# Gate/value passes on two row halves over 128 columns instead of four quarters of the array

## The chip, the cores and the metric

The kernel runs on one core of a Trainium2 chip. A core has TensorE (matrix products; the profile shows its matmuls as PE and its weight loads as PEld), VectorE (DVE), ScalarE (ACT), GpSimd (POOL) and SyncE (SP), which run side by side and wait for each other by semaphores. The metric is device time in microseconds (us) for one execution. Smaller is better.

## The reference, cut to what matters

There are 8 batches, 12 heads, 448 rows and a head dimension of 64. Squared-ReLU attention is followed by a gated feed-forward layer of width 1536.

```python
scores = scale * np.matmul(q, k.transpose(0, 1, 3, 2))      # per batch and head: 448 x 448
attn   = np.maximum(scores, 0.0) ** 2 / S
x      = np.matmul(attn, v)                                  # -> 3584 rows x 768
gate   = np.maximum(x @ w_gate, 0.0)                         # 768 x 1536
val    = x @ w_val
out    = gate * val @ w_out                                  # 1536 x 768
```

The kernel works in bf16 with sums in fp32.

## The kernel before

**One batch after the other, two in a pair.** For each batch the kernel makes three kinds of products: score tiles (21 of them, each two 64-row strips of keys of four heads against 448 queries), value products (3, of 7 steps each) and gate/value units (12, one for each block of 128 of the 1536 columns). For each pair of batches `out_pair` then makes the output product. The last pair's gate/value work is another function, `gv_pair`, which forms sums of blocks first and needs fewer products.

**How a product lies in the array.** TensorE holds a stationary operand of up to 128 rows by 128 columns and streams the moving operand past it. A head has only 64 elements, so two row halves of the array do different work: rows 0 to 63 belong to one half of the partitions, rows 64 to 127 to the other. `mm4` (L79) cuts the columns in two as well. For each row half `r` and column half `c` it issues one matmul of 64 rows by 64 columns, so one *pass* is four weight loads and four matmuls, one for each quarter of the array:

```python
for r, p in HALVES:
    for c, half in HALVES:
        mm(o[r][half], lhs(r, c)[p], rhs(r, c)[p], start, stop)
```

The two row halves write to two different PSUM banks `o[0]` and `o[1]`, the two column halves to partitions 0 to 63 and 64 to 127 of each. Scores (`tile_of`, L242), values (`value_passes`), gate/value units (`gv_unit`, L302) and `gv_pair` (L500) all use `mm4`. In scores and values the two column halves hold different weights and also stream different data (`c` picks another pair of heads). In a gate/value pass both column halves stream the same `x`, and their weights are two neighbouring blocks of 64 columns.

**A gate/value unit** fills two banks: one with the gate, one with the value, each 128 columns by 448 rows of `x`. Partitions 0 to 63 of the weights `gv_sb` hold `w_gate`, partitions 64 to 127 hold `w_val`. `x` exists twice, with even and odd heads exchanged between the halves of the partitions, so that each weight half meets each head. That gives 12 passes (6 pairs of heads, twice), each over all 448 rows of `x`. After the last pass ScalarE takes the ReLU of the gate bank and VectorE multiplies it with the value bank.

**Other shapes of the array.** The output products (`out_pair`, L355), the transposes of the first two batches (L208, L217) and the idle matmuls at the start use 128 rows by 64 columns, two matmuls side by side.

**The order of TensorE's work** is written out: every instruction is kept in program order. `spread` (L702) runs through the passes of the 12 units of one batch and puts *events* between them: score tiles and value products of the next batch, placed by `paced` (L740) at even distances. So a gate/value stretch of a few passes alternates with one score tile (one pass of four matmuls) or one value product (seven passes). `first_batch` (L609) has an order of its own, written out by hand, in which score tiles, transposes, value products and the first gate/value passes alternate. ScalarE and VectorE turn each score tile into squared ReLU (L232, L233).

Of the kernel before, what the change touches and what calls it, by code (L numbers as in the profile page):

```python
# [16 lines left out]
def kernel(  # L17
# [24 lines left out]
    B, H, S, D = q.shape  # L42
# [23 lines left out]
    HALVES = [(c, slice(c * 64, c * 64 + 64)) for c in range(2)]  # L66

    def pin(ins):
        return tc.keep_in_program_order(ins)

    def mm(o, l, r, start, stop):
        pin(nc.tensor.matmul(o, lhsT=l, rhs=r, start=start, stop=stop, skip_group_check=True))  # L72
# [6 lines left out]
    def mm4(o, lhs, rhs, start, stop):  # L79
# [4 lines that stand above are left out]
# [10 lines left out]
    def pair_of(b, slot):  # L94
        qd, c = divmod(slot, 2)
        return slot if b == 0 else qd + c * NQ
# [205 lines left out]
    def gv_unit(b, mf, order, take):  # L302

        hT = hT_of[b - b % 2]
        c0 = CHUNK_OF[mf]
        w = gv_sb[c0]
        f = mf * 128 - CHUNKS[c0][0]
        col = (b % 2) * S
        o = []

        def step(n, e, hp):
            if n == 0:
                ps = take()
                o.extend(ps[:, r, :S] for r in range(2))
            x = x_of[b][e][hp // 2]
            mm4(o, lambda r, c: w[:, 2 * pair_of(b, hp) + (r ^ e), f + c * 64:f + c * 64 + 64], lambda r, c: x[:, hp % 2, :],
                n == 0, n == H - 1)
            if n == H - 1:
                g_sb = gpool.tile([128, S], BF16, name="g_sb")
                pin(nc.scalar.activation(g_sb, o[0], AF.Relu, scale=float(out_scale)))  # L320
                pin(nc.vector.tensor_tensor(hT[:, mf, col:col + S], o[1], g_sb, ALU.mult))  # L321
        return [lambda n=n, e=e, hp=hp: step(n, e, hp) for n, (e, hp) in enumerate(order)]
# [538 lines left out]
```

## Time and profile before

| | |
|---|---|
| median of 2 runs | 400.27 us (399.39 to 401.15) |
| the profiled execution | 400.31 us, span 398.5 us |
| TensorE clock granted | 0.999 of full speed |
| TensorE busy | 98% of the span, 7376 matmuls and 7376 weight loads |
| weight loads (PEld) busy | 70% |
| VectorE, ScalarE, GpSimd busy | 76%, 61%, 24% |

By stage the span divides like this:

| stretch, us | what runs |
|---|---|
| 0 to 38.3 | first batch: transposes, its attention, the first gate/value passes |
| 38.3 to 100.4 | gate/value of batches 0 and 1, attention of batches 1 and 2 |
| 100.4 to 124.4 | output product of the first pair |
| 124.4 to 197.6 | gate/value of batches 2 and 3, attention up to part of batch 5 |
| 197.6 to 221.6 | output product of the second pair |
| 221.6 to 297.5 | gate/value of batches 4 and 5, the rest of the attention |
| 297.5 to 321.5 | output product of the third pair |
| 321.5 to 369.7 | gate/value of the last pair (`gv_pair`) |
| 369.7 to 398.5 | output product of the last pair |

In a line of the profile's groups, `64*64 64x448` after a matmul means that 64 rows and 64 columns of the array are in use and that 64 partitions of 448 elements stream in; then come the count, the busy time of the group and the mean duration of one. Several matmuls run at once and a matmul's duration includes its way through the array, so durations don't add up to time. In a line of the timeline the first number is the start in us from the span's start, the second the time until the last of the merged instructions ends, then engine, line, operation, names of what is written and read, shapes, and `x` with the number of instructions.

### The profile page before, as it was taken

The page shows a single profiled execution, that of the slowest core. Times are in us where ns is not written, and L with a number is a line of the kernel's source. Part 1 is how long each engine was busy: PE and PEld are TensorE (multiplying, and loading weights), DVE is VectorE, ACT ScalarE, POOL GpSimd, SP SyncE. Part 2 cuts the span into 40 slices and gives each one's busy share as a digit, 9 for nine tenths or more (in the row PEclk, how much of TensorE's full clock was granted, in tenths as well). Part 3 has the DMA queues.
Part 4 walks back from the last instruction along what each step waited for, and adds up shares of the span by engine and source line. Part 5 has one row for each costly group of instructions (what it writes and reads, how often), then busy time and mean ns, then how long its engine had stood idle before and what let it go on. Part 6 is the DMA issues. An engine that isn't in the chain of part 4 may idle for free.

```text
span 398.5 us, 16574 instructions
## 1 busy us (share of the span) xinstructions
PE 389.0 (98%) x7376; PEld 278.4 (70%) x7376; DVE 303.4 (76%) x530; ACT 243.6 (61%) x358; POOL 96.9 (24%) x168
## 2 busy tenths in 40 slices
PE   7799999999999999999999999999999999999995
PEld 4477777778776666666677666988887766777664
DVE  5975886599944686887882578888889869997922
ACT  4962994787334786988732788899873233444231
POOL 8933300810214600503041260020003120000213
PEclk9999999999999999999999999999999999999999
DMA  9999998999736794995963497760002350000135
GB/s 153 177 197 196 196 181 107 156 205 179 138 86 180 89 179 86 148 151 76 161 157 95 130 125 107 112 83 2 3 3 60 77 145 3 3 2 3 22 91 169
DMA packets 90872, 44.17 MB, mean 111 GB/s; under 512 B 55424, under 2 KB 89792, under 8 KB 90800
## 3 DMA queue, kind: packets, MB, share of 16 engines
q0 software_dynamic: 51264, 28.83, 50.5%
q1 hardware_dynamic: 39104, 13.99, 18.8%
q8 instruction: 57, 0.93, 0.9%
q10 hardware_dynamic: 432, 0.30, 0.3%
q14 instruction: 15, 0.12, 0.1%
HBM read 47.19 MB, written 11.01 MB: 146 GB/s over the span
## 4 chain that ended last, share of the span: by engine, by line
PE 93%; DVE 3%; DMA 1%; POOL 1%; issue 0%; ACT 0%; POOLq 0%; ACTq 0%
PE ps L72 92%; DVE attn L233 2%; DMA qn<-in_q_dram 1%; PE ps L208 1%; DVE kqT L209 1%; POOL qn L116 0%; ACT r_sb L232 0%; POOL kn L116 0%; DVE x L653 0%; DVE attn L399 0%; POOL ident L112 0%; POOLq L112 0%; ACTq L232 0%; POOLq L845 0%
## 5 line engine op out<-in xcount | busy, mean ns | idle before, releaser
L72 PE MATMUL ps<-x,gv 64*64 64x448 bf16 x3408 | 197.7, 349 | 0.4 <-ACT r_sb L232 0.3
L72 PEld LDWEIGHTS <-gv 64*64 64x64 bf16 x4032 | 140.2, 107 | 53.2 <-issue 2.2
L232 ACT ACTIVATE r_sb<-ps 128x896 bf16<-128x896 f32 x167 | 148.9, 933 | 16.9 <-PE ps L72 14.6
L233 DVE TENSOR_TENSOR attn<-r_sb 128x896 bf16<-128x896 bf16 x167 | 101.9, 622 | 30.0 <-ACT r_sb L232 23.2
L409 POOL DMA_DIRECT2D out_dram<-attn x63 | 33.1, 531 | 167.6 <-DVE attn L399 132.8
L72 PEld LDWEIGHTS <-hT 128*64 128x64 bf16 x1056 | 55.8, 110 | 21.0 <-issue 1.4
L72 PE MATMUL ps<-kqT 64*64 64x448 bf16 x672 | 66.1, 351 | 3.0 <-ACT r_sb L232 2.6
L395 ACT ACTIVATE attn<-ps 128x384 f32<-128x384 f32 (+1 forms) x64 | 28.8, 450 | 64.3 <-PE ps L72 63.8
L72 PE MATMUL ps<-wo,hT 128*64 128x384 bf16 (+1 forms) x720 | 54.3, 306 | 0.0
L321 DVE TENSOR_TENSOR hT<-ps,g_sb 128x448 bf16<-128x448 f32 x72 | 44.5, 619 | 8.0 <-ACT g_sb L320 7.4
L320 ACT ACTIVATE g_sb<-ps 128x448 bf16<-128x448 f32 x72 | 39.2, 546 | 17.2 <-PE ps L72 16.9
L399 DVE TENSOR_TENSOR attn<-ps,attn 128x384 f32<-128x384 f32 (+1 forms) x48 | 22.8, 503 | 32.5 <-ACT attn L395 17.8
L72 PEld LDWEIGHTS <-vn 64*64 64x64 bf16 (+1 forms) x888 | 34.4, 107 | 12.5 <-issue 1.2
L72 PE MATMUL ps<-attn,vn 64*64 64x448 bf16 x672 | 37.2, 349 | 0.0
L72 PEld LDWEIGHTS <-kqT 64*64 64x64 bf16 x672 | 25.9, 106 | 14.8 <-issue 5.3
L528 ACT ACTIVATE kqT<-ps 128x896 f32<-128x896 f32 x18 | 16.5, 918 | 25.0 <-PE ps L72 25.0
L116 POOL DMA_DIRECT2D vn<-in_v_dram x36 | 23.7, 683 | 17.3 <-DMA wo<-in_moe_w_out_dram 9.5
L72 PE MATMUL ps<-o_ring,hT 128*64 128x384 bf16 (+1 forms) x336 | 26.0, 306 | 0.0
L691 POOL COPY flag<-kqT 128x1 bf16<-128x1 bf16 x12 | 2.8, 253 | 88.7 <-DMA kqT<-kr 66.0
L532 DVE TENSOR_TENSOR kqT<-ps,kqT 128x896 f32<-128x896 f32 x18 | 19.5, 1086 | 5.9 <-PE ps L72 4.2
L261 DVE COPY x<-x 64x896 bf16<-64x896 bf16 x34 | 13.8, 405 | 1.8
L116 POOL DMA_DIRECT2D qn<-in_q_dram x20 | 14.8, 765 | 1.3 <-POOLq L845 0.8
(101 smaller groups left out, 288.3 us busy)
## 6 DMA issues: line engine op xcount, KB each, us to landing
out_dram<-attn POOLq DMA_DIRECT2D x48, 96.0 KB, 2.5
out_dram<-attn SPq DMA_DIRECT2D x48, 96.0 KB, 2.6
kn<-in_k_dram POOLq DMA_DIRECT2D x7, 384.0 KB, 6.9
qn<-in_q_dram POOLq DMA_DIRECT2D x7, 384.0 KB, 9.2
vn<-in_v_dram POOLq DMA_DIRECT2D x14, 192.0 KB, 9.2
gv<-in_moe_w_gate_dram POOLq DMA_DIRECT2D x6, 384.0 KB, 11.9
gv<-in_moe_w_val_dram POOLq DMA_DIRECT2D x6, 384.0 KB, 12.1
wo<-in_moe_w_out_dram POOLq DMA_DIRECT2D x2, 1152.0 KB, 13.8
```

The lines of the kernel that those rows point to most:

```text
L72: pin(nc.tensor.matmul(o, lhsT=l, rhs=r, start=start, stop=stop, skip_group_check=True))
L116: pin(nc.gpsimd.dma_start(out=o, in_=i))
L232: pin(nc.scalar.activation(r, src, AF.Relu))
L233: pin(nc.vector.tensor_tensor(dst, r, r, ALU.mult))
L261: pin(nc.vector.tensor_copy(x1[p], x0[other]))
L320: pin(nc.scalar.activation(g_sb, o[0], AF.Relu, scale=float(out_scale)))
L321: pin(nc.vector.tensor_tensor(hT[:, mf, col:col + S], o[1], g_sb, ALU.mult))
L395: pin(nc.scalar.activation(out_of(t, r, c), bank(P, t), AF.Copy))
L399: pin(nc.vector.tensor_tensor(o, bank(Q, t), o, ALU.add))
L409: pin(engines[c].dma_start(out=rows[:, c0:c1, :], in_=src))
L528: pin(nc.scalar.activation(held(n, j), both(PQ[n][0]), AF.Copy))
L532: pin(nc.vector.tensor_tensor(k, both(PQ[n][1]), k, ALU.add))
```

## The change

In a unit's pass, `mm4` goes and a loop over the two row halves takes its place. Each row half now does one matmul of 64 rows by 128 columns: one weight load of 128 columns and one matmul that writes all 128 partitions of its bank. The products and the order of the passes stay the same. Scores, values and `gv_pair` keep `mm4`.

```diff
@@ -313,8 +313,9 @@
                 ps = take()
                 o.extend(ps[:, r, :S] for r in range(2))
             x = x_of[b][e][hp // 2]
-            mm4(o, lambda r, c: w[:, 2 * pair_of(b, hp) + (r ^ e), f + c * 64:f + c * 64 + 64], lambda r, c: x[:, hp % 2, :],
-                n == 0, n == H - 1)
+            head = 2 * pair_of(b, hp)
+            for r, p in HALVES:
+                mm(o[r], w[p, head + (r ^ e), f:f + 128], x[p, hp % 2, :], n == 0, n == H - 1)
             if n == H - 1:
                 g_sb = gpool.tile([128, S], BF16, name="g_sb")
                 pin(nc.scalar.activation(g_sb, o[0], AF.Relu, scale=float(out_scale)))
```

## The prediction

> **What bounds the kernel now.** I read the page first: busy times, the chain that ended last, the costliest groups.
>
> ```profile
> PE 389.0 (98%) x7376; PEld 278.4 (70%) x7376; DVE 303.4 (76%) x530; ACT 243.6 (61%) x358; POOL 96.9 (24%) x168
> ...
> PE 93%; DVE 3%; DMA 1%; POOL 1%; issue 0%; ACT 0%; POOLq 0%; ACTq 0%
> ...
> L72 PE MATMUL ps<-x,gv 64*64 64x448 bf16 x3408 | 197.7, 349 | 0.4 <-ACT r_sb L232 0.3
> L72 PEld LDWEIGHTS <-gv 64*64 64x64 bf16 x4032 | 140.2, 107 | 53.2 <-issue 2.2
> ```
>
> TensorE is busy for 98% of the span and holds 93% of the chain; the gate/value matmuls waited 0.4 us in all. The answer on who waited for whom adds up TensorE's waits to 5.2 us, 3.0 of them score tiles waiting for ScalarE early on. So the time is TensorE's order of work, and only what lengthens or shortens that order counts.
>
> A mean of 349 ns for a matmul is not what it costs: they overlap. The cost is the distance between starts, so next came the timeline of TensorE in a full stretch:
>
> ```profile
> 151.16 0.36 PE L72 MATMUL ps<-kqT 64*64 64x448 bf16 x4
> 151.35 1.30 PE L72 MATMUL ps<-x,gv 64*64 64x448 bf16 x24
> 152.49 0.36 PE L72 MATMUL ps<-kqT 64*64 64x448 bf16 x4
> 152.68 1.30 PE L72 MATMUL ps<-x,gv 64*64 64x448 bf16 x24
> ```
>
> 24 gate/value matmuls, six passes of four quarters, take 152.49 - 151.35 = 1.14 us, 0.190 a pass; single starts say 189.1 ns, the four of a pass within 11 ns, each one's next weight load starting 2 ns behind it. The score tile between them costs one more pass (151.16 to 151.35) and nothing for the change of work: scores, values and gate/value passes all use the array as four quarters of 64 by 64.
>
> **What it removes.** Each of 72 units (6 batches, 12 blocks of 128 columns) has 12 passes: 864 passes. Four matmuls and four weight loads of each become two: 1,728 fewer of either. What is a pass then? In the output products a pass is two matmuls over 384 columns, and their starts lie 162.5 ns apart in the trace. 64 columns fewer save 26.6 ns, so 0.416 ns a column: 448 columns are 186.5, and about 2.5 ns remain in both forms, with four instructions as with two. So **halving the number of instructions buys nothing** that the rows show: a pass stays 189 ns. At the very best the 2.5 ns go, 864 x 2.5 = 2.2 us; that is the bound below nothing, and I take 0. The halves should run beside each other: today quarters of both row halves start 4 to 11 ns apart and write the same partitions of two banks, which is what two halves need.
>
> **What it adds: changes of the array's shape.** Scores and values stay on quarters while the gate/value passes around them become halves. The spreading places these in the middle of the passes: 21 score tiles and 3 value products for each of seven batches are 168 interruptions, the first batch has 2 more (at 23.4 and 25.1 us), and in the trace each stands alone between gate/value passes. That is 170 changes into quarters and 170 back: 2 before 38.3 us, 48 from there to 100.4, 56 from 124.4 to 197.6, 64 from 221.6 to 297.5. What one costs, the trace shows only for another pair of shapes: near 32 us transposes (128 rows by 64 columns) interrupt gate/value passes (64 by 64).
>
> ```profile
> 31.82 0.41 PE L208 MATMUL ps<-ident,kn 128*64 128x128 bf16 x8
> 32.07 0.39 PE L208 MATMUL ps<-ident,qn 128*64 128x128 bf16 x8
> 32.29 0.39 PE L208 MATMUL ps<-ident,kn 128*64 128x128 bf16 x8
> 32.52 0.39 PE L208 MATMUL ps<-ident,qn 128*64 128x128 bf16 x8
> 32.84 0.95 PE L72 MATMUL ps<-x,gv 64*64 64x448 bf16 x16
> 33.72 0.41 PE L208 MATMUL ps<-ident,kn 128*64 128x128 bf16 x8
> ```
>
> From 31.82 to 33.72 is 1.90 us. Inside are 16 pairs of transposes at 56 ns (0.224 for 8 matmuls, as from 32.07 to 32.29), 0.896 us, and four gate/value passes, 0.757. **0.247 us are left for two changes of shape**; the next cycle, 33.72 to 35.61, leaves 0.24. I take 0.245. The single starts say how it is made up: the first load of the new shape starts 91 to 95 ns after the last column of the old shape went in (otherwise it starts a pass ahead), and the first pass of the new shape is 24 ns too long, since its load lies open. At 100.4 us, from quarters to the output products, it is the same: 309 ns where 189 are the step, and 24 more.
>
> Whether a change between 64 by 64 and 64 by 128 costs this too, no row shows. Bounds: nothing, if the next load goes in behind the running pass as it does within a shape; and 0.28 us if the array finished the whole last matmul (349 ns by its row) and then loaded openly (107 ns by its row): 349 + 107 + 11 - 189. 340 changes make that 0 to 95 us. I take the row of the other shapes, 0.1225 each, since it is the only change of shape in the trace and came out the same in both directions and in both kinds of work. For the change into halves I add 24 ns: the open load of 64 columns showed 24, and 128 columns at the same rate show 48.
>
> On this step the Trainium skill has a rule, "TensorEngine Tiling (Array Packing)", Key Properties: to change the tiling mode, and not merely the tile, drains TensorE; its list of configurations has 64×128 and 64×64 as different modes. The trace agrees for 128 by 64 against 64 by 64, at 0.12 us; for the pair at hand no run shows it yet. By the rule the sum below stands, without it nothing is added.
>
> **Hidden or not.** TensorE waits for nobody in these stretches, so the pauses fall on the path in full. One further change, into halves at 22.6 us, lies under a wait for ScalarE (0.35 us) and costs nothing. The three stretches of transposes and the five edges of output products change shape today and will after. ScalarE and VectorE do the same work in more time; DMA transfers get more room. If the pauses let ScalarE run ahead, at most the 3.0 us of score waits shrink, and those are nearly all before 22 us, ahead of the added changes.
>
> **Sum.** 170 x (0.245 + 0.024) = 45.7 us. The profiled execution took 400.31 us, its span 398.5 and 1.8 around it; the median of the two runs is 400.27, the same. 400.3 + 45.7 = **446 us**, by stage +0.5, +12.9, +15.1 and +17.2.
>
> **The rivals.**
> - *No pause between these two shapes: 400 us.* Row halves are the same in both shapes, only the columns join, and the load could go into spare weights while the other pass streams. For it: within one shape this happens in every pass. Against: the loads were held back at every change of shape that the trace has. It ends on the other side, not slower: 398 to 402. It decides below 8 us / 340 = 24 ns a change, a fifth of the row.
> - *The loads bound the half passes.* A load of 64 columns has 107 ns in its row; if 128 columns have 214, and a half can't take its next weights sooner, a pass is 214 + 2 ns in place of 189: 864 x 27 = 23 us, thus 423 without pauses and 469 with them. Against: the transposes get a new 64-column load every 56 ns, so most of the 107 is not occupancy, and at a change a load shows 24. A pause in one direction alone gives 170 x 0.1225 = 21 us, 421, too.
> - *The two halves run one after the other* (it doesn't do what it says): 864 x 0.189 = 163 us more, 563 or above. Against: the quarters of two row halves do run together.
> - *Faster by over 2%* needs 8 us; passes can give 2.2 and waits 5.2 in all, of which those of the first microseconds stay.
>
> On the loads the skill's "TensorE: Matmul & The Clock Gate", LDWEIGHTS, estimates a load as columns / 1.2 in ns, 53 ns for 64 and 107 for 128. By that estimate two loads of 128 columns fit into 189 ns if they run beside each other and not one after the other (214). The trace shows four loads of 64 per pass starting within 12 ns and holding up nothing.
>
> **How the numbers follow.** Pauses as in the row, 432 to 460 us: 0.65. Pauses and loads together, or longer pauses, about 469: 0.08. Loads alone or a pause one way, 421 to 423: 0.06. No pause, 400: 0.17. Halves in turn, 563: 0.02. Faster by over 2%: 0.02. The range leaves out the last three (0.21) and takes in the others: 418 to 472. The far end of the pause's price (0.28 each, 495) is left outside, since both directions of the row lie under half of it. A measurement of this kernel tells some 2% (8 us) from no change; so faster 0.02, same 0.17, slower 0.81.
>
> **What would show it.** Gate/value matmuls as 64*128, 1,728 of them, and 5,648 on TensorE in all. In the timeline a score tile's four matmuls are followed by the next pass after some 0.30 to 0.32 us in place of 0.19, the first half pass lasts some 0.24, and the last one before a score tile 0.29; half passes between them still 0.189. The output products and the last pair's stretch (321.5 to 369.7 us) keep their lengths. TensorE may still count as busy near 98%, because a matmul's 349 ns cover the pause. I am wrong if 0.19 stays across the change (first rival), or if the half passes themselves grow (second).

## The result and the profile after

The changed kernel takes 437.75 us (436.75 to 438.75), the kernel before 400.27: a ratio of 1.092, 95% interval 1.087 to 1.097. It is slower by 37.5 us. Forecast were 446 us, range 418 to 472.

The page of the changed kernel: busy times, the chain that ended last, and the groups of the changed passes, of the gate/value weight loads and of the loads for score tiles.

```profile
PE 425.7 (98%) x5648; PEld 220.6 (51%) x5648; DVE 306.0 (70%) x530; ACT 248.8 (57%) x358; POOL 96.7 (22%) x168
...
PE 94%; DVE 3%; DMA 1%; ACT 0%; issue 0%; DVEq 0%; ACTq 0%
...
L72 PE MATMUL ps<-x,gv 64*128 64x448 bf16 (+1 forms) x1776 | 193.8, 351 | 0.3 <-ACT r_sb L232 0.3
...
L72 PEld LDWEIGHTS <-gv 64*128 64x128 bf16 (+1 forms) x2304 | 89.6, 97 | 94.1 <-issue 38.8
...
L72 PEld LDWEIGHTS <-kqT 64*64 64x64 bf16 x672 | 19.3, 103 | 61.1 <-issue 59.1
```

1,728 matmuls and as many loads fewer, and TensorE is still "busy" for 98%: the added time (the span grew by 36.5 us) is not idle time by the page, since a matmul's recorded duration (351 ns by its row) reaches over the pause behind it (at a change, starts lie 282 to 316 ns apart). The page shows it only at the weight loads: those of the score tiles waited 59.1 us for "issue", that is for nothing that the profile shows, and those of the gate/value passes 38.8. On the page before, it was 5.3 us for the score tiles (2.2 for the gate/value passes), since the loads went in a pass ahead:

```profile
L72 PEld LDWEIGHTS <-kqT 64*64 64x64 bf16 x672 | 25.9, 106 | 14.8 <-issue 5.3
```

The timeline shows where the time is. TensorE in a full stretch of the changed kernel (start, time to the last end, what ran):

```profile
150.28 1.50 PE L72 MATMUL ps<-x,gv 64*128 64x448 bf16 x14
151.71 0.38 PE L72 MATMUL ps<-kqT 64*64 64x448 bf16 x4
152.02 1.31 PE L72 MATMUL ps<-x,gv 64*128 64x448 bf16 x12
153.26 0.38 PE L72 MATMUL ps<-kqT 64*64 64x448 bf16 x4
153.58 0.74 PE L72 MATMUL ps<-x,gv 64*128 64x448 bf16 x6
```

Six half passes and a score tile take from 151.71 to 153.26, 1.55 us. The same seven passes took 1.33 before (151.16 to 152.49). From the score tile to the next half pass it is 0.31 to 0.32, where it was 0.19. The single starts in the trace say how the 0.23 us are made up. They have hardly any spread:

| step between starts | before | after | more |
|---|---|---|---|
| half pass to half pass (quarter to quarter before) | 189.2 ns | 189.2 ns | 0 |
| last half pass to score tile | 189 | 282.5 | 93 |
| score tile to first half pass | 189 | 316 | 127 |
| first half pass to second | 189 | 200 | 11 |

That is **231.5 ns for each interruption** by work in quarters, and 170 interruptions make 39.4 us. By stretch (edges in the trace: last transposes, output products), with what is left of the length after 189.2 ns for each pass:

| stretch | length before, after | more | left over before, after | changes of shape x 115.8 ns |
|---|---|---|---|---|
| transposes of batch 1 to first output product | 63.8, 72.8 us | 9.1 | 2.1, 11.2 | 96: 11.1 |
| first to second output product | 73.1, 86.0 | 12.9 | 0.1, 13.0 | 112: 13.0 |
| second to third | 75.9, 90.5 | 14.6 | 0.2, 14.9 | 128: 14.8 |

The output products, 23.9 us each from the first to the last matmul start (24.3 the last), and the last pair's stretch between them (48.3 us) are as they were. The leftover of the changed kernel is the changes of shape, to within 0.1 us. The 2.4 us that were left over before are gone: single passes of the kernel before were held up there, most of them ahead of a value product or a score tile, and the pauses now give that time anyway.

### The profile page after: what moved, and what is told of

It is laid out like the page before. It is cut to its first block, busy times and chain, and to the rows that moved or that the text cites. A ratio compares the mean times of both kernels' runs of the same rounds, so it can differ in the third digit from the quotient of the medians.

```text
span 435.0 us, 13118 instructions
## 1 busy us (share of the span) xinstructions
PE 425.7 (98%) x5648; PEld 220.6 (51%) x5648; DVE 306.0 (70%) x530; ACT 248.8 (57%) x358; POOL 96.7 (22%) x168
## 4 chain that ended last, share of the span: by engine, by line
PE 94%; DVE 3%; DMA 1%; ACT 0%; issue 0%; DVEq 0%; ACTq 0%
PE ps L72 93%; DVE attn L233 2%; DMA kr<-in_k_dram 1%; PE ps L208 1%; DVE kqT L209 1%; PE ps L217 0%; ACT r_sb L232 0%; DVE r_sb L631 0%; DVE x L654 0%; DVE attn L633 0%; DVE kn L128 0%; DVE attn L400 0%; DVEq L128 0%; ACTq L232 0%
## 5 line engine op out<-in xcount | busy, mean ns | idle before, releaser
L72 PE MATMUL ps<-x,gv 64*128 64x448 bf16 (+1 forms) x1776 | 193.8, 351 | 0.3 <-ACT r_sb L232 0.3
L232 ACT ACTIVATE r_sb<-ps 128x896 bf16<-128x896 f32 x167 | 150.9, 928 | 40.7 <-PE ps L72 38.7
L72 PEld LDWEIGHTS <-gv 64*128 64x128 bf16 (+1 forms) x2304 | 89.6, 97 | 94.1 <-issue 38.8
L72 PE MATMUL ps<-kqT 64*64 64x448 bf16 x672 | 63.5, 372 | 2.9 <-ACT r_sb L232 2.6
L72 PEld LDWEIGHTS <-kqT 64*64 64x64 bf16 x672 | 19.3, 103 | 61.1 <-issue 59.1
L321 ACT ACTIVATE g_sb<-ps 128x448 bf16<-128x448 f32 x72 | 38.8, 540 | 18.6 <-PE ps L72 17.8
L72 PEld LDWEIGHTS <-vn 64*64 64x64 bf16 (+1 forms) x888 | 28.4, 107 | 19.7 <-issue 7.8
L266 ACT ACTIVATE x<-ps 128x448 bf16<-128x448 f32 x14 | 7.6, 544 | 15.5 <-PE ps L72 15.5
```

The source lines that it names most:

```text
L232: pin(nc.scalar.activation(r, src, AF.Relu))
```

## The experiments

**The score tiles in halves too.** If the change of shape costs, then it must go away where the neighbours take the same shape, although there are more half passes.

```diff
-        mm4([ps[:, r, :S] for r in range(2)], lambda r, c: T[:, 0, pair_of(b, 2 * qd + c), a:a + 64],
-            lambda r, c: T[:, 1, pair_of(b, 2 * qd + c), :], True, True)
+        hp, a = pair_of(b, 2 * qd + i % 2), min(a, S - 128)
+        for r, p in HALVES:
+            mm(ps[:, r, :S], T[p, 0, hp, a:a + 128], T[p, 1, hp, :], True, True)
```

> The changed kernel with the score tiles in halves too: each row half takes 128 keys of one head in place of 64 keys of two heads (other products than the reference's, as many passes, the same amount written). Only the value products are left in quarters. Theory (a pause at every change of shape, 232 ns for a pair of changes in the changed kernel's trace): of 170 interruptions of half passes 21 value products stay, and 4 parts of value products in the first batch now stand between half passes, 25 x 0.232 = 5.8 us over the kernel before; with up to 3 us of older waits again hidden under them 403 to 407 us. Rival (the half passes themselves are dear, 37.5 us / 864 = 43 ns each): 168 more of them, 437.8 + 7 = 445 us.

Measured: 403.6 us, 1.006 of the kernel before (1.004 to 1.009). TensorE's timeline in that run:

```profile
155.46 0.35 PE L72 MATMUL ps<-kqT 64*128 64x448 bf16 x2
155.65 1.87 PE L72 MATMUL ps<-x,gv 64*128 64x448 bf16 x18
157.45 1.52 PE L72 MATMUL ps<-attn,vn 64*64 64x448 bf16 x28
158.90 1.88 PE L72 MATMUL ps<-x,gv 64*128 64x448 bf16 x18
```

A score tile goes into the half passes within one step again (155.46 to 155.65). The value product, still in quarters, costs what a change costs: nine half passes take 1.80 (155.65 to 157.45) in place of 1.70, seven value passes 1.45 in place of 1.32. Half passes as such are not dear, or this run would have been the slowest so far.

**All in halves.** The value products as well.

```diff
-            mm4([ps[:, r, :S] for r in range(2)], lambda r, c: v_sb[:, 2 * qd + c, i, :],
-                lambda r, c: attn[:, 2 * i + c, :], i == 0, i == NC - 1)
+            c, j = i % 2, min(i, NC - 2)
+            for r, p in HALVES:
+                mm(ps[:, r, :S], v_sb[p, 2 * qd + c, j:j + 2, :].rearrange("p i d -> p (i d)"), attn[p, 2 * i + c, :],
+                   i == 0, i == NC - 1)
```

> As the run with the scores in halves, and the value products in halves as well (each row half takes 128 columns of one head pair in place of 64 of two; other products than the reference's, as many passes). Nothing that interrupts the half passes has another shape now. Theory (change of shape): no added pause is left, 400 us within 1% (398 to 403). Rival (half passes dear, 43 ns each): 864 + 336 of them, 400.3 + 52 = 452 us.

Measured: 400.8 us, ratio 1.000 (0.997 to 1.003). TensorE's timeline in that run:

```profile
150.74 0.35 PE L72 MATMUL ps<-kqT 64*128 64x448 bf16 x2
150.93 1.30 PE L72 MATMUL ps<-x,gv 64*128 64x448 bf16 x12
152.06 0.35 PE L72 MATMUL ps<-kqT 64*128 64x448 bf16 x2
```

Seven passes take 1.32 us, with two instructions of each kind per pass as with four. Between the first and the second output product 384 of the 385 steps lie at 188 to 190 ns, one at 201. So 1,200 passes in halves cost exactly what they cost in quarters, and the whole 37 us belong to the mixture.

**Halves and quarters in turn.** Half the half passes, two and a half times the changes.

```diff
+            if n % 2 == 0:
+                head = 2 * pair_of(b, hp)
+                for r, p in HALVES:
+                    mm(o[r], w[p, head + (r ^ e), f:f + 128], x[p, hp % 2, :], n == 0, n == H - 1)
+            else:
+                mm4(o, ...)
```

> Gate/value passes with an even number in a unit in halves, with an odd number in quarters; scores and values in quarters. Half as many half passes as in the changed kernel (432), five times as many changes of shape (each pass ends in one, some 863). Theory (pause at each change, 0.116 us): 863 x 0.116 = 100 us, some 497 to 501 us. Rival (half passes dear): 432 x 0.043 = 19 us, 419 us. Rival (it costs only where a score tile or value product interrupts): at most the changed kernel's time, 438 us.

Measured: 497.4 us (one run), at a granted clock of 0.998. The trace has 859 changes. The "five times" of the expectation sets changes against the 170 interruptions; against the 340 changes of the changed kernel it is 2.5 times. Its sum, 863 x 0.116, doesn't depend on that. Steps from half to quarters took 293 ns, from quarters to half 316, together 231 over two plain passes; 432 such pairs make 99.8 us; the span is 97.1 longer than that of the kernel before, the rest being old holds that the pauses take over. The time follows the number of changes over a factor of 2.5, and the price of one stays.

**Score tiles in twos, in the changed kernel.** The same passes, fewer interruptions.

```diff
+        i = 0
+        while i + 1 < len(events):
+            if events[i][3] == events[i + 1][3] == 1:
+                places[i] = (*places[i + 1][:2], places[i][2])
+                i += 1
+            i += 1
         return places
```

> The changed kernel with two score tiles in a row at one place wherever two follow each other in the plan: some 63 of the 170 interruptions fall away, the same passes are made. Theory (pause at each change): 63 x 0.232 = 14.6 us less, 437.8 - 14.6 = 423 us (421 to 426, if ScalarE keeps up with two tiles in a row). Rival (half passes dear, or each score tile dear by itself): 438 us.

Measured: 424.0 us, 1.057 of the kernel before (1.054 to 1.059). The trace has 107 interruptions, 63 fewer. In the timeline two tiles follow each other with one pause for both:

```profile
159.66 2.44 PE L72 MATMUL ps<-x,gv 64*128 64x448 bf16 x24
162.04 0.57 PE L72 MATMUL ps<-kqT 64*64 64x448 bf16 x8
162.54 1.31 PE L72 MATMUL ps<-x,gv 64*128 64x448 bf16 x12
```

From 162.04 to 162.54 is 0.50 us, two passes (0.38) and 0.12 for the change back with the open load of the first tile.

**The same twos in the kernel before**, by the same edit, as the control.

> The kernel before with the score tiles in twos as in the run of the changed kernel with pairs. It has no change of shape at these places. Theory (what the pairs won there was pauses alone): the kernel before stays at 400 us within 1%, or a little above where ScalarE is late for the second tile. Rival (each interruption costs by itself, whatever the shape): some 14 us less, 386 us.

Measured: 409.0 us, 1.018 (1.014 to 1.023). That is neither: pairing doesn't gain anything in quarters, it loses 7.7 us (the kernel before took 401.3 in this set of runs). TensorE's timeline in that run, around one value product:

```profile
236.01 1.11 PE L72 MATMUL ps<-x,gv 64*64 64x448 bf16 x20
237.01 0.38 PE L72 MATMUL ps<-kqT 64*64 64x448 bf16 x4
237.20 0.57 PE L72 MATMUL ps<-x,gv 64*64 64x448 bf16 x8
237.82 1.52 PE L72 MATMUL ps<-attn,vn 64*64 64x448 bf16 x28
```

Two passes from 237.20 take 0.62 in place of 0.38: the value product is held for 0.24 us. And ScalarE's timeline there:

```profile
236.04 2.54 ACT L232 ACTIVATE r_sb<-ps 128x896 bf16<-128x896 f32 x3
```

ScalarE works through three score tiles in a row, and score tiles and value products share two pairs of banks. The second of the three ends at 237.77 in the trace, 0.05 before the value product starts. Such holds, of value products and of score tiles, come to 4.8, 1.8 and 4.0 us in the three stretches, against 2.1, 0.1 and 0.2 in the kernel before; that all of them come from ScalarE is inferred from this one. In the changed kernel with twos the leftover is nearly all changes of shape (60, 70 and 80 of them, 6.9, 8.1 and 9.3 us, of 7.9, 8.4 and 9.9): its pauses hide the same lateness. Pairing as such wins nothing, and the changes that fell away (126 x 0.116 = 14.6 us) account for the gain of 14 us there.

**One pass of both shapes.** Two accounts are left of why a change costs: the array holds one shape at a time, or loads of another shape must not overtake a pass on the same rows. In batch 4 a pass is made a half on rows 0 to 63 and two quarters on rows 64 to 127.

```diff
+            (_, p), (_, q) = HALVES
+            mm(o[0], w[p, head + e, f:f + 128], x[p, hp % 2, :], n == 0, n == H - 1)
+            for c, half in HALVES:
+                mm(o[1][half], w[q, head + (1 ^ e), f + c * 64:f + c * 64 + 64], x[q, hp % 2, :], n == 0, n == H - 1)
```

> The kernel before, with the passes of batch 4 alone (144) mixed within themselves: rows 0 to 63 as one half of 128 columns, rows 64 to 127 as two quarters. The three matmuls of a pass use no row in common with the other shape. Theory (the pause belongs to the array as a whole: one shape at a time): the half and the quarters go one after the other with a pause at either, 289 + 309 ns = 598 in place of 189, 144 x 0.409 = 59 us, some 459 us. Rival (the pause only guards rows that change shape themselves, as a weight load must not overtake a pass on the same rows): rows 64 to 127 stay in quarters all the time and rows 0 to 63 change only at the 31 or so interruptions of batch 4, at most 31 x 0.232 = 7 us, 400 to 408 us.

Measured: 520.6 us (one run). The expectation of 459 was passed by 61 us, for a reason that neither account had: the granted clock. The busy times by stretch, with batch 4 from 221.6 us on (length, busy time and number for PE, PEld, DVE, ACT and POOL, granted clock, DMA share, GB/s):

```profile
221.60:260.00 38.40, 38.40 (x152) 9.23 (x151) 7.07 (x12) 8.96 (x11) 7.13 (x13) 0.57 0.51 74
260.00:300.00 40.00, 40.00 (x169) 9.91 (x167) 7.58 (x14) 8.44 (x11) 0.00 (x0) 0.54 0.00 1
300.00:340.00 40.00, 40.00 (x163) 9.59 (x161) 9.45 (x17) 8.48 (x11) 0.85 (x3) 0.50 0.16 35
340.00:380.00 40.00, 40.00 (x188) 10.52 (x190) 8.10 (x14) 9.09 (x13) 2.16 (x4) 0.50 0.15 18
380.00:420.00 40.00, 40.00 (x822) 32.81 (x816) 33.61 (x61) 34.14 (x50) 0.00 (x0) 0.99 0.01 3
```

In the 5 us before the clock fell the starts are 222.719 (half), 223.009 (quarters), 223.318 (half), 223.607, 223.917: 289 and 309 ns, a pass of 599 ns. That is what the first account gave (598), three times a plain pass. At half the clock the steps are 482 and 515 ns. The array as a whole keeps to one shape here; but most of these passes ran at half the clock, so the dose was taken down:

> The kernel before, with one pass in each of the 72 units (the seventh of twelve) mixed as in the run with mixed passes: rows 0 to 63 as one half, rows 64 to 127 as two quarters. Theory (one shape at a time in the whole array): at each the half runs alone between two pauses and the quarters of the other rows follow, 0.189 + 0.232 = 0.42 us, 72 x 0.42 = 30 us, some 431 us, at a granted clock near 1. Rival (the pause only guards the rows that change): rows 64 to 127 go on, at most 72 x 0.232 = 17 us where the order of issue holds them up too, 400 to 417 us.

```diff
-            if b == 4:
+            if n == 6:
```

Measured: 427.7 us (one run) at a granted clock of 1.000, 26.9 over the kernel before of the same set of runs (400.9). The account of one shape at a time gave 30, the other at most 17. Between the first and the second output product, where hardly any old holds lie, 24 such passes add 9.8 us, 0.41 each where 0.42 were expected. The starts of one such pass are 61.651 (quarters), 61.933 (half), 62.221 (quarters of the other rows): 282 and 288 ns, although no row of the last two is shared. So rows that keep their shape wait too. A half lies over all 128 columns, so the two always share columns; whether a part of the array with neither rows nor columns in common would wait, no run shows.

**Half of the rows without work.** Was it the idle half of the array that took the clock down?

```diff
+            if b == 4:
+                for c, half in HALVES:
+                    mm(o[0][half], w[0:64, head + e, f + c * 64:f + c * 64 + 64], x[0:64, hp % 2, :], n == 0, n == H - 1)
```

> The kernel before, with the gate/value passes of batch 4 on rows 0 to 63 alone, in two quarters (the value half of these passes is left out). No shape changes and no pause. In the run with mixed passes the granted clock fell to 0.5 for 150 us from a few us after the start of batch 4. Theory (it falls because too little of the array is at work, here half of the rows): clock 0.5 in batch 4's stretch of some 38 us, a pass 0.376 in place of 0.189, up to 144 x 0.187 = 27 us and the scores in it, 427 to 437 us. Rival (half of the rows is not enough for it, the pauses have to come on top): clock near 1, 400 us.

Measured: 401.0 us (one run), clock 0.997 in all and 1.00 in that stretch. Half the rows alone don't do it, and pauses alone don't either (0.998 with halves and quarters in turn). Both together did. It need not be the pair as such. An estimate from the steps, for gate/value passes alone: each row half streams 0.32 of the time in the mixed passes (189 of 599 ns) and 0.62 with halves and quarters in turn (189 of 305), and with half the rows at work the array streams at 0.5 on average. A count of the array's use with a limit between 0.32 and 0.5 would fit as well. What exactly the throttle counts stays open.

**96 of 128 columns**, for the one price that was forecast too high: the open load of a half pass, 11 ns and not 48.

```diff
-                mm(o[r], w[p, head + (r ^ e), f:f + 128], ...
+                mm(o[r][0:96], w[p, head + (r ^ e), f:f + 96], ...
```

> The changed kernel with 96 of the 128 columns in each half pass (a quarter of the gate and value columns is left out); shape of the array, passes and moving columns stay. In the changed kernel's trace the first half pass after a change is 11 ns too long, the first quarter pass 24, though its load has half the columns; and the load of 128 columns reads its weights as four strips of 32. Theory (the strips load the weights in a fraction of the time, and 96 columns are loaded one by one): the first half pass is 36 ns too long (24 x 96 / 64), 170 x 0.025 = 4 us more, 442 us. Rival (the open load costs a half pass 11 ns in any form): 438 us, and 200 ns for the first half pass.

Measured: 441.3 us (one run); the first half pass takes 226.7 ns, 37.5 too long where 36 were expected. In the trace the three stretches are together 4.2 us longer than in the changed kernel. The groups of weight loads, first of the changed kernel, then of this one (busy, mean ns of one, idle time before):

```profile
L72 PEld LDWEIGHTS <-gv 64*128 64x128 bf16 x1728 | 70.1, 94 | 86.1 <-issue 38.5
...
L72 PEld LDWEIGHTS <-gv 64*64 64x64 bf16 x576 | 19.5, 107 | 8.0 <-issue 0.3
```

```profile
L72 PEld LDWEIGHTS <-gv 64*96 64x96 bf16 x1728 | 92.3, 119 | 72.8 <-issue 38.5
```

128 columns have 94 ns, 64 have 107, 96 have 119. 96 lie 12 ns above 64, as column by column would have it (32 x 0.416 = 13); 128 lie below both. The load of 128 columns reads four strips of 32, the others one strip. The Trainium skill describes this in "TensorE: Matmul & The Clock Gate", Weight-path perf modes: loads of 128 columns that are not fp32 read their weights as four chunks side by side. The numbers here agree: 11 ns open in place of 24 and 37.5.

## Why the prediction was right, point by point

- **What bounds it**: TensorE's order of work. Right; after the change TensorE is busy for 98% of the span and holds 94% of the chain.
- **Fewer instructions buy nothing**: right. A pass has 189.2 ns in halves and quarters, and with all work in halves the time is 1.000 of before.
- **The halves run beside each other**: right, their starts lie 3 to 4 ns apart.
- **170 interruptions**: right, the trace has 170.
- **The price of a change, taken from the transposes**: right in kind, and right in size into quarters (118 ns with the open load, 122.5 forecast). Into halves 146.5 were forecast and 114 measured. The step that failed in size is the 24 ns that were *added* for a load of 128 columns; it should have been 13 *less* than a load of 64, since such a load goes in four strips and lies open for 11 ns; with 96 columns, in one strip, it is 37.5. Here the prediction carried the rate of one strip over to 128 columns. 170 x 37 ns make 6.3 of the 9.2 us between the forecast 45.7 and the 36.5 that the span grew by.
- **"TensorE waits for nobody in these stretches"**: nearly. The list of waits has only times in which no matmul was running by its record, and a record of 349 ns covers a hold of up to 160. The steps over 189 ns show 2.4 us of holds in the three stretches, which the pauses took over. The first 38 us end no later than before: there the pauses of the two interruptions (0.46 us) took over a hold of 0.22, and the first gate/value pass started 0.26 us earlier in this execution, which is chance as far as the traces show. These 0.46 and 2.4 us are the other 2.9: 39.4 - 36.5.
- **The rivals**: no pause (400) is excluded by the trace's steps, and the run with all in halves shows that the added time goes with the mixture. Loads as the bound (423, 469): half passes keep 189 ns even with the slower 96-column loads. Halves one after the other: excluded by the steps.
- **The rule on tiling modes**: the Trainium skill, "TensorEngine Tiling (Array Packing)", Key Properties, says that a change of tiling mode drains TensorE. The traces agree for this pair of shapes: 116 ns a change on average. The runs with mixed passes show that even rows that keep their shape have to wait.

## What to carry to other kernels

Where passes of several kinds alternate on TensorE, the shape of the array is part of the schedule: keep one shape for all that alternates, even if that takes twice the instructions, and let shapes change only at the edges of long stretches. A price for a change can be read where two shapes meet in a trace, here even another pair of shapes (0.245 us for two changes, 0.2315 for the pair that was asked): take the distance between starts less the plain step, not the idle time, which hides it. Count the changes before the passes: 170 interruptions at 0.23 us (39.4 us) outweighed everything that 864 passes could have given (2.2).

## What was not expected of the hardware

- A weight load of 128 columns is quicker than one of 64: 94 against 107 ns in the records, and 11 against 24 ns open at a change. One of 96 is slower than both (119 and 37.5).
- With half the rows at work at a time and a pause at every step, the granted clock fell to 0.5 for 150 us, 5.6 us after this began, with one rise of 3.4 us between. Half the rows without pauses kept it at 1.00, full passes with pauses at 0.998.
- Two score tiles in a row cost the kernel before 7.7 us (409.0), while its list of waits names only 1 us more for ScalarE (4.0 against 3.0): holds that are shorter than a matmul's record don't appear there.
